# A tile of its own for the weights of q and k, and the first unit's maxima among the last projections

## The chip, the core and the metric

The kernel runs on one core of one Trainium2 chip. A core has five engines that run beside each other, each through its own list of instructions in order: TensorE (PE, with its weight loads as PEld), VectorE (DVE), ScalarE (ACT), GpSimd (POOL) and SyncE (SP), which here issues nearly all DMAs. The metric is the device time of one execution in microseconds (us), the median of several runs. In the profile a tile is named by its program name (`khat`, `rl`, `pm`); nearly all instructions are recorded through one helper, so the profile gives line 76 for all of them, and one goes by tiles.

## The reference

Two independent results are put side by side, 448 columns each, for 2048 positions, all in 32-bit floats:

```python
P = exp((A * dt)[:, :, None] * pos)          # A complex, 448 channels x 256 states
K = 2 * einsum("dn,dnl->dl", C, P).real      # a convolution kernel of 2048 for each channel
y = irfft(rfft(u_t, 4096) * rfft(K, 4096))[:, :, :2048] + u * D_skip

q, k, v = split(x @ wqkv)                    # 16 heads of 28
p = softmax(q @ k.T * 28 ** -0.5)
b = (p @ v) @ wo
```

## The kernel before, in words

**Opening stage** (lines 213 to 565). It makes two things and writes both to DRAM. One is q, k and v: x is turned on PE in four chunks of 512 rows (`transposes`, line 433), split into a rounded part `xh` and a rest `xl`, and multiplied by the weights, split in the same way. A q or k projection (`qk_proj`, line 443) is twelve matmuls of 512 columns into one bank of PSUM, for one chunk and one group of four heads; ScalarE and VectorE then split the result into `hl`, which is written out. A v projection (`v_proj`, line 475) is twelve matmuls too, evacuated by ScalarE. There are 12 projections a chunk, 48 in all; all take their bank from one ring of three (`w_tile`, line 126). The other thing is the *seeds*: for eight blocks of 56 channels (`seeds`, line 314) exponentials and sines on ScalarE, reductions and small products on VectorE (`g_first`, line 400), factors on POOL (`factors`, line 381). These make the tables from which the main loop builds powers of exp(A dt).

A seed block is thirteen steps, and a block begins every four slots (`SP`), so that there are 41 slots; the projections are spread over the first 37 (`PW`). Loads for the main loop are put into slots by `ahead` and the constants `A0`, `A1`, `KW` (line 44). In this stage the written order is only a priority: a scheduler orders the instructions of each engine when the kernel is built. The chip then follows that order, engine by engine.

The weights of q and k lie in the tile `khat` (`k0_t`, lines 135 and 233), in which the first group's keys are to lie later: four parts of 1 MB, one for each head slot `j`, each loaded by four DMAs of 256 KB (`load_k`, line 146). The weights of group `j` lie in part `j`, so a part can be loaded when all the projections of its group are done. x, v's weights and small tiles lie in the pool `y_p` (line 218).

**First maxima** (lines 537 to 562). Softmax takes an upper bound of each row's maximum off the scores. For a unit (four heads and 512 queries; there are 16 units) it is found by scores on PE, with one difference of keys for each pair of chunks (`kdif`): max(a, b) = b + relu(a - b). For the first unit this is done after the stage, 16 times: five matmuls into two tiles of two banks, a Relu of 128x1024 on ScalarE and an add-and-maximum of 128x1024 on VectorE. One matmul takes the negated q (`nq`, made by POOL). The 16 maxima are then turned by PE, split by VectorE into `mh` and written into spare rows of `qhat` by a DMA (`max_end`, `max_put`, lines 199 and 207), so that the score matmul subtracts them itself.

**Main loop** (from line 878). 256 steps, 16 for each unit, with an order that is written out by hand and kept as written (`ORDER`): scores, exponentials and sums of one unit, the maxima of the next, and the convolution's work in between. It reads the first seeds (`sdb`), `qhat` and `khat` at its start.

Pools lie in memory as stacks, some from the left, some from the right end: a pool that opens where another was closed waits for the users of the old tiles. A tile of a pool with several buffers waits for the last use of the buffer that it gets.

Of the kernel before, what the change touches and what calls it, by code (L numbers as in the profile page):

```python
# [8 lines left out]
F32 = mybir.dt.float32  # L9
# [8 lines left out]
L = 2048  # L18
# [3 lines left out]
DH = 28  # L22
# [21 lines left out]
A0, A1, KW = 26, 34, (33, 35, 36)  # L44
# [47 lines left out]
def body(ctx, tc, a, out):  # L92
# [41 lines left out]
    k0_p = pool(k0_st, "k0_p", side="right")  # L134
    k0_t = k0_p.tile([128, HG, L], F32R, name="khat")
# [10 lines left out]
    def load_k(g, j, p):  # L146
        if j == 0:
            t = k0_t if g == 0 else p.tile([128, HG, L], F32R, name="khat")
# [64 lines left out]
    with ExitStack() as st:  # L213
        sst, xst, wst, mst, psx, psm = (ExitStack() for _ in range(6))
# [3 lines left out]
        y_p = pool(wst, "y_p", side="right")  # L218
# [17 lines left out]
        nc.gpsimd.memset(k0_t[:CK].rearrange("p g (n e) -> p (g n) e", e=32)[:, :, DH:].bitcast(F32), 0.0)  # L236
# [16 lines left out]
        def load_nat(o):  # L253
            nats[o] = s_p.tile([PO, 4, 256], F32, name="nat", bufs=2)
# [178 lines left out]
        def transposes(c):  # L433
            for k in range(NCK):
                pt = ps_t.tile([128, CQ], F32, name="pt")[:CK]
                for t in range(4):
                    nc.tensor.transpose(pt[:, t * 128:(t + 1) * 128], xns[c, t // 2][:, t % 2, k * CK:(k + 1) * CK], ident)
                xh[k] = x_p.tile([CK, CQ], F32R, name="xh", bufs=XB)
                xl[k] = x_p.tile([CK, CQ], F32R, name="xl", bufs=XL)
                nc.scalar.activation(xh[k], pt, AF.Copy)  # L440
                nc.vector.tensor_tensor(xl[k], pt, xh[k].bitcast(F32), ALU.subtract)
# [47 lines left out]

        work = []  # L490
# [23 lines left out]
        for j, t in enumerate(KW):  # L514
            ahead[t].append(lambda j=j: load_k(0, j, k0_p))

        def project():

            e = work.pop(0)() if work else None
            while pend:  # L520
                pend.pop(0)()
            if e:
                pend.append(e)

        for t in range(n_stage):
# [4 lines left out]
            if t + 1 == PW:  # L530
                project()
                wst.close()
                load_k(0, HG - 1, k0_p)
                load_q(1)
                for c in range(NQ):
                    load_v(0, c)
        xst.close()
        psx.close()
        m_p = pool(mst, "m_p")
        ps_2 = pool(psm, "ps_2", 4, PSUM)  # L540
        nq = m_p.tile([128, HG, CQ], F32R, name="nq")
        m_u[0, 1] = q_p.tile([128, HG * 4], F32, name="m1", bufs=2)
        for i in range(16):
            j, t = divmod(i, 4)
            ts = slice(t * 128, (t + 1) * 128)
            q, kt = q_u[0][:, j, ts], kt_g[0][j]
            if t == 0:
                nc.gpsimd.tensor_scalar(nq[:, j], q_u[0][:, j].bitcast(F32), -1.0, None, op0=ALU.mult)
            pd, pb = (ps_2.tile([128, 2, CQ], F32, name="p2") for _ in range(2))
            kb = kt.rearrange("p (c s n) -> p c s n", c=NQ, s=2)[:, :2, 1, :]  # L550
            mm = nc.tensor.matmul
            mm(pd[:, 0], q, kd_g[0, j], start=True, stop=True)
            mm(pd[:, 1], q, kt[:, 2 * CQ:3 * CQ], start=True, stop=False)
            mm(pd[:, 1], nq[:, j, ts], kt[:, 3 * CQ:], start=False, stop=True)
            mm(pb[:, 0].rearrange("p (c n) -> p c n", c=2), q, kb, start=True, stop=True)
            mm(pb[:, 1], q, kt[:, 3 * CQ:], start=True, stop=True)
            rl = m_p.tile([128, 2, CQ], F32, name="rl2", bufs=2)
            nc.scalar.activation(rl, pd, AF.Relu)
            nc.vector.tensor_tensor_reduce(rl, pb, rl, 1.0, -3.0e38, ALU.add, ALU.max, m_u[0, 1][:, i:i + 1])
        nc.scalar.activation(half_pi[:1], half_pi[:1], AF.Exp)  # L560
        max_end(0, ps_2.tile([128, 2, CQ], F32, name="p2")[:, 0])
        max_put(0)
        psm.close()
        mst.close()
# [12 lines left out]
    k_pools = [k0_p, kq_p]  # L577
# [580 lines left out]
```

## Time and profile before

| what | value |
| --- | --- |
| median of three runs | 1303.82 us (1302.89 to 1305.15) |
| the profiled execution | 1307.74 us |
| its span, first to last instruction | 1305.7 us |
| mean clock of PE | 0.976 |
| PE busy from 0 to 180 us, in stretches of 20 us | 12.06 to 18.74 us |
| PE busy from 260 to 300 us | 39.45 us |
| bytes moved by DMA | 205.28 MB, mean 157 GB/s |

The span is the profile's own, and the time beside it is that of the same execution. Engine rows give a start, a duration, the operation, out<-in, and in brackets the idle time before it and what ended it. The chain of waits is followed back from the last instruction: each piece is released by the one before it.

### The profile page before, as it was taken

The numbers are of one execution on the slowest core, as the hardware profiler recorded it, in microseconds if no ns is written. First come the engines' busy times: TensorE is split into PE (matmuls) and PEld (weight loads), VectorE is DVE, ScalarE is ACT, GpSimd is POOL, SyncE is SP. The second block draws the span as 40 slices with busy tenths as digits, with TensorE's granted clock in tenths as the row PEclk, the third lists the DMA queues.
The fourth block names the chain that finished last, engine by engine and source line by source line (L and its number), as shares of the span: only waits on it lengthen the run. The fifth ranks groups of instructions, "written<-read, shape, count | busy, mean of one in ns | idle before, by whom it ended". The sixth has DMA issues, their size and how long they took to land.

```text
span 1305.7 us, 32148 instructions
## 1 busy us (share of the span) xinstructions
PE 1228.7 (94%) x12193; PEld 695.7 (53%) x12193; DVE 907.0 (69%) x2001; ACT 980.3 (75%) x2046; POOL 865.9 (66%) x684
## 2 busy tenths in 40 slices
PE   6888877799999999999999999999997999999998
PEld 5766755355555555555555555555554555545333
DVE  5676656677777787777788888888986555636111
ACT  4877875588888888888788888888886666756463
POOL 2677654478888788888769999999995221424421
PEclk9989887799999999999999999999999999999999
DMA  6677679735866455468634232743324453647666
GB/s 202 207 273 257 218 259 271 212 66 136 185 147 142 109 149 157 142 169 231 162 104 105 56 83 62 157 111 78 82 59 139 146 158 136 203 142 238 202 161 175
DMA packets 200082, 205.28 MB, mean 157 GB/s; under 512 B 95992, under 2 KB 158520, under 8 KB 197880
## 3 DMA queue, kind: packets, MB, share of 16 engines
q1 hardware_dynamic: 199864, 203.22, 56.1%
q8 instruction: 96, 1.57, 0.5%
q14 instruction: 58, 0.48, 0.1%
q10 hardware_dynamic: 64, 0.02, 0.0%
HBM read 120.74 MB, written 82.18 MB: 155 GB/s over the span
## 4 chain that ended last, share of the span: by engine, by line
PE 72%; POOL 8%; ACT 7%; DVE 5%; DMA 4%; issue 4%; SPq 0%; ACTq 0%; POOLq 0%
PE pm L76 39%; PE pss L76 16%; PE po L76 16%; POOL sg L76 2%; POOL e L76 2%; DMA khat<-k 2%; POOL tri L76 2%; ACT tri L76 1%; ACT sg L76 1%; DVE mx L76 1%; POOL p L76 1%; ACT L76 1%; ACT p L76 1%; POOL eu L76 1%; DVE rl L76 1%
## 5 line engine op out<-in xcount | busy, mean ns | idle before, releaser
L76 ACT ACTIVATE p<-pss 128x512 f32<-128x512 f32 x1024 | 560.4, 609 | 109.9 <-PE pss L76 105.9
L76 PE MATMUL pss<-qhat,khat 128*128 128x512 f32 x1024 | 405.7, 402 | 4.0 <-DMA qhat<-mh 2.2
L76 DVE TENSOR_REDUCE mx<-pm 128x1 f32<-128x512 f32 x480 | 308.3, 683 | 121.2 <-PE pm L76 119.5
L76 PE MATMUL pm<-khat,qhat 128*128 128x512 f32 x720 | 314.4, 437 | 6.1 <-ACT rl L76 3.5
L76 POOL TENSOR_TENSOR e<-e,sdb 128x256 f32<-128x256 f32 x168 | 202.0, 1203 | 108.7 <-ACT e L76 67.2
L76 PE MATMUL po<-p,v 128*32 128x512 f32 x2048 | 271.0, 597 | 0.0
L76 POOL TENSOR_TENSOR e<-e,eu 128x256 f32<-128x256 f32 x168 | 248.3, 1478 | 13.2
L76 PEld LDWEIGHTS pm<-khat,qhat 128*128 128x128 f32 x720 | 135.4, 188 | 206.4 <-ACT p L76 47.0
L76 PEld LDWEIGHTS pss<-qhat,khat 128*128 128x128 f32 x1024 | 191.2, 189 | 52.5 <-ACT p L76 13.8
L76 DVE CUSTOM_DVE_ANT_0 rl<-pm,rl 128x512 f32<-128x512 f32 x240 | 165.3, 689 | 70.0 <-ACT rl L76 67.7
L76 POOL TENSOR_TENSOR eu<-e,sdb 128x256 f32<-128x256 f32 x168 | 202.3, 1204 | 0.0
L76 POOL TENSOR_TENSOR p<-pr,pr 64x448 f32<-64x448 f32 x64 | 73.2, 1144 | 155.6 <-PE pm L76 122.3
L76 DVE TENSOR_TENSOR g<-g,zg 128x128 f32<-128x128 f32 x392 | 162.0, 413 | 3.6
L76 ACT ACTIVATE rl<-pm 128x512 f32<-128x512 f32 x240 | 145.3, 605 | 7.7 <-issue 4.1
L76 PE MATMUL pm<-xh,khat 112*128 112x512 f32 x256 | 89.7, 431 | 19.6 <-DVE hl L76 10.6
L76 PE MATMUL pm<-kdif,qhat 128*128 128x512 f32 x240 | 97.0, 404 | 1.7 <-DVE pr L76 1.1
L76 DVE TENSOR_TENSOR zg<-g,zg 128x128 f32<-128x128 f32 x224 | 88.0, 393 | 5.3
L76 PEld LDWEIGHTS pm<-e,g 128*32 128x32 f32 x3584 | 56.9, 110 | 49.2 <-issue 15.7
L76 PE MATMUL pm<-e,g 128*32 128x64 f32 x3584 | 73.6, 223 | 8.7 <-POOL e L76 8.7
L76 ACT ACTIVATE y<-pm 128x448 f32<-128x448 f32 x48 | 26.5, 553 | 59.7 <-PE pm L76 39.1
L76 PEld LDWEIGHTS pm<-xh,khat 112*128 112x128 f32 x256 | 51.0, 205 | 35.9 <-DVE hl L76 12.6
L76 DVE TENSOR_TENSOR pr<-pm,ub 128x448 f32<-128x448 f32 x64 | 37.0, 619 | 46.9 <-PE pm L76 37.7
(133 smaller groups left out, 1491.6 us busy)
## 6 DMA issues: line engine op xcount, KB each, us to landing
sdb<-sd SPq DMA_DIRECT2D x56, 336.0 KB
khat<-k SPq DMA_DIRECT2D x64, 256.0 KB
qhat<-q SPq DMA_DIRECT2D x64, 256.0 KB
sd<-sg SPq DMA_DIRECT2D x8, 1456.0 KB
k<-hl SPq DMA_DIRECT2D x16, 512.0 KB
q<-hl SPq DMA_DIRECT2D x16, 512.0 KB
v<-v SPq DMA_DIRECT2D x32, 256.0 KB
mw<-in_mw SPq DMA_DIRECT2D x16, 512.0 KB
```

The lines of the kernel that those rows point to most:

```text
L76: i = f(*args, **kw)
```

## The change

- The weights of q and k get a tile `w` of their own in a new pool on the left side. The pool of the first keys, `k0_p`, is opened only in the course of the last projections, after `y_p` has been closed, and lies where `y_p` was.
- The rests `xl` of three of the four parts of x lie in tiles of v's pool instead of a pool of their own; a `nat` tile is 128 rows high, so that the negated q can lie in it.
- In the last chunk the keys of the first group are projected first, then v, then the others.
- From the 41st projection on, a plan `MG` gives for each the part of the keys to load and the first unit's maxima to compute after it: parts 2, 3, 0, 1 after projections 41 to 44, and from 43 on two maxima after each; the rest follows after the stage.
- Each maximum is done in two halves of 512 columns: each has a tile of one bank for the difference (`pt`, two buffers, that of the transposes) and one of the ring of three for the added part, a Relu of 128x512, and an add-and-maximum of 128x512 into a column of its own. One more reduction joins the halves at the end.
- The differences of keys and the first q are loaded in earlier slots (`A0` 26 to 18, `A1` 34 to 28).

```diff
-A0, A1, KW = 26, 34, (33, 35, 36)
+A0, A1 = 18, 28
+MG = {41: (2, ()), 42: (3, ()), 43: (0, (8, 9)), 44: (1, (10, 11)), 45: (None, (12, 13)), 46: (None, (14, 15)), 47: (None, (0, 1)),
+      48: (None, (2, 3)), 49: (None, (4, 5)), 50: (None, (6, 7))}
...
-    k0_p = pool(k0_st, "k0_p", side="right")
-    k0_t = k0_p.tile([128, HG, L], F32R, name="khat")
...
+        w_p = pool(wst, "w_p")
+        y_p = pool(yst, "y_p", side="right")
...
-        w_g = k0_t[:CK].rearrange("p g (i s k h e) -> p i s k g h e", i=2, s=2, k=NCK, h=HG)
+        w_t = w_p.tile([CK, HG, L], F32R, name="w")
+        w_g = w_t.rearrange("p g (i s k h e) -> p i s k g h e", i=2, s=2, k=NCK, h=HG)
...
+        xls = [v_p.tile([128, NK // NQ, HG, 32], F32, name="v", bufs=5).rearrange("p t h e -> p (t h e)")[:CK].bitcast(F32R) for _ in range(3)]
+        xls.append(x_p.tile([CK, CQ], F32R, name="xl"))
...
+        def max_group(i):
+
+            j, t = divmod(i, 4)
+            ts = slice(t * 128, (t + 1) * 128)
+            if not nqs:
+                m_u[0] = q_p.tile([128, HG, 4, 3], F32, name="mx", bufs=2)
+            if t == 0:
+                if j % 2 == 0:
+                    nq = s_p.tile([128, 4, 256], F32, name="nat", bufs=2).rearrange("p (j a) n -> p j (a n)", j=2).bitcast(F32R)
+                    nqs[j], nqs[j + 1] = nq[:, 0], nq[:, 1]
+                nc.gpsimd.tensor_scalar(nqs[j], q_u[0][:, j].bitcast(F32), -1.0, None, op0=ALU.mult)
+            q, kt = q_u[0][:, j, ts], kt_g[0][j]
+            kb = kt.rearrange("p (c s n) -> p c s n", c=NQ, s=2)[:, :2, 1, :]
+            mm = nc.tensor.matmul
+            for h in range(2):
+                pd, pb = ps_t.tile([128, CQ], F32, name="pt"), w_tile()
+                if h == 0:
+                    mm(pd, q, kd_g[0, j], start=True, stop=True)
+                    mm(pb.rearrange("p (c n) -> p c n", c=2), q, kb, start=True, stop=True)
+                else:
+                    mm(pd, q, kt[:, 2 * CQ:3 * CQ], start=True, stop=False)
+                    mm(pd, nqs[j][:, ts], kt[:, 3 * CQ:], start=False, stop=True)
+                    mm(pb, q, kt[:, 3 * CQ:], start=True, stop=True)
+                rl = kd_p.tile([128, CQ], F32, name="rl", bufs=2)
+                nc.scalar.activation(rl, pd, AF.Relu)
+                nc.vector.tensor_tensor_reduce(rl, pb, rl, 1.0, -3.0e38, ALU.add, ALU.max, m_u[0][:, j, t, h:h + 1])
+
+        def first_maxima(n):
+
+            j, ts = plan.pop(n, (None, ()))
+            if j is not None:
+                if not k0:
+                    yst.close()
+                    k0.append(pool(k0_st, "k0_p", side="right"))
+                load_k(0, j, k0[0])
+            for i in ts:
+                groups.remove(i)
+                max_group(i)
...
-            jobs = v_jobs + jobs if c == NQ - 1 else jobs + v_jobs
+            jobs = jobs[:1] + v_jobs + jobs[1:] if c == NQ - 1 else jobs + v_jobs
...
-        for j, t in enumerate(KW):
-            ahead[t].append(lambda j=j: load_k(0, j, k0_p))
...
+            first_maxima(n_work - len(work))
...
-                load_k(0, HG - 1, k0_p)
...
+            elif t + 1 > PW:
+                first_maxima(n_work + t + 1 - PW)
+        while groups:
+            max_group(groups.popleft())
```

More of the change, by code (lines that the diff above doesn't have):

```diff
@@ L146, in load_k @@
     def load_k(g, j, p):
-        if j == 0:
-            t = k0_t if g == 0 else p.tile([128, HG, L], F32R, name="khat")
+        if g not in kt_g:
+            t = p.tile([128, HG, L], F32R, name="khat")
             kt_g[g] = [t[:, i] for i in range(HG)]
@@ L213, in body @@
     with ExitStack() as st:
-        sst, xst, wst, mst, psx, psm = (ExitStack() for _ in range(6))
+        sst, xst, wst, yst, psx = (ExitStack() for _ in range(5))
+        k0 = []
         t_p = pool(sst, "t_p")
@@ L438, in transposes @@
                 xh[k] = x_p.tile([CK, CQ], F32R, name="xh", bufs=XB)
-                xl[k] = x_p.tile([CK, CQ], F32R, name="xl", bufs=XL)
+                xl[k] = xls[k]
                 nc.scalar.activation(xh[k], pt, AF.Copy)
@@ L488, in v_proj @@
             return evac
+        nqs, plan = {}, dict(MG)
+        groups = collections.deque([j * 4 + t for j in (2, 3, 0, 1) for t in range(4)])
+        def max_group(i):
[33 more added lines that the diff above has]
+                max_group(i)
         work = []
@@ L536, in body @@
                     load_v(0, c)
+            elif t + 1 > PW:
+                first_maxima(n_work + t + 1 - PW)
+        while groups:
+            max_group(groups.popleft())
+        nc.scalar.activation(half_pi[:1], half_pi[:1], AF.Exp)
+        m_u[0, 1] = q_p.tile([128, HG * 4], F32, name="m1", bufs=2)
+        nc.vector.tensor_reduce(m_u[0, 1], m_u[0].rearrange("p a b c -> p (a b) c")[:, :, :2], axis=AX.X, op=ALU.max)
+        max_end(0, ps_t.tile([128, CQ], F32, name="pt"))
+        max_put(0)
         xst.close()
         psx.close()
[L539 to L564, printed above, removed]
         sst.close()
```

7 lines of the change are left out of this document (3 added, 4 removed).

## The prediction

> **What bounds the kernel now.** I read the page first: the span, the busy time of each engine, and PE's share slice by slice.
>
> ```profile
> span 1305.7 us, 32148 instructions
> PE 1228.7 (94%) x12193; PEld 695.7 (53%) x12193; DVE 907.0 (69%) x2001; ACT 980.3 (75%) x2046; POOL 865.9 (66%) x684
> PE   6888877799999999999999999999997999999998
> ```
>
> From the ninth slice on (a slice is 32.6 us) TensorE is busy nine tenths and more: the main loop. I compared the order of instructions in the two kernels: from the main loop's first instructions to the end it is the same on all five engines. So only the opening stage, some 245 us, can change. I read that stage in windows (stretch, length, busy PE, PEld, DVE, ACT, POOL with their counts, clock, DMA share, GB/s), and then in the chain of work that ended last.
>
> ```profile
> 180.00:190.00 10.00, 4.84 (x12) 3.84 (x13) 8.55 (x13) 4.68 (x9) 5.32 (x5) 0.66 0.44 167
> 190.00:200.00 10.00, 7.26 (x25) 5.38 (x24) 1.44 (x2) 9.91 (x13) 4.38 (x3) 0.83 1.03 291
> 200.00:210.00 10.00, 2.86 (x8) 2.03 (x7) 5.38 (x11) 2.57 (x8) 7.84 (x8) 0.66 1.08 263
> ```
> ```profile
> 208.44 9.86 DMA khat<-k
> 218.32 10.46 DMA khat<-k
> 228.92 3.26 PE p L76 x12
> ...
> 235.65 0.02 DVE m L76
> ...
> 236.38 5.56 DMA qhat<-mh
> ...
> 242.00 2.99 DMA sdb<-sd
> ...
> 245.15 0.63 ACT e L76
> ```
>
> From 180 to 210 one engine at a time is near full and the others wait for it. From 208.44 to 228.79 the chain is the load of the first keys. The last maximum is done at 235.67, and the main loop's first work on ScalarE starts at 245.15, 9.5 us later. The change acts on what comes before 235.67.
>
> **The change part by part.** *What it removes.* The first keys no longer wait for weights in the same tile. Without their loads the old maxima would still have to run:
>
> ```profile
> L76 DVE CUSTOM_DVE_ANT_0 rl<-p,rl 128x1024 f32<-128x1024 f32 x16 | 19.2, 1224 | 8.3 <-ACT rl L76 7.8
> L76 DVE DVE_READ_ACCUMULATOR2_ANT m<- 128x1 f32 x16 | 1.3, 83 | 0.0
> L76 ACT ACTIVATE rl<-p 128x1024 f32<-128x1024 f32 x16 | 16.3, 1026 | 10.9 <-PE p L76 10.4
> ```
>
> 16 x (1.224 + 0.083) = 20.9 us of VectorE from about 208 would end near 229: the loads cost at most 235.7 - 229 = 7 us. What is gained beyond that must come from maxima beside projections.
>
> *What it adds.* 32 halves of 128x512 stand for 16 maxima of 128x1024. The main loop has both instructions:
>
> ```profile
> L76 DVE CUSTOM_DVE_ANT_0 rl<-pm,rl 128x512 f32<-128x512 f32 x240 | 165.3, 689 | 70.0 <-ACT rl L76 67.7
> L76 ACT ACTIVATE rl<-pm 128x512 f32<-128x512 f32 x240 | 145.3, 605 | 7.7 <-issue 4.1
> L76 ACT ACT_TABLE_LOAD x4 | 5.1, 1283 | 0.1
> ```
>
> VectorE: 32 x (0.689 + 0.083) = 24.7 us, 3.8 more. ScalarE: 32 x 0.605 = 19.4, 3.0 more. Matmuls (80) and negations of q (four) stay. The new order also holds 23 activation table loads instead of 17: 6 x 1.283 = 7.7 us more on ScalarE, because Exp and Sin alternate inside the later seed blocks. The Trainium skill, ScalarE: Activation LUTs, section "Table sets: the hidden batching unit", asks to batch activations by table set, which speaks against this order; the price here is the row's, so the rule alters nothing in the sum.
>
> *What it moves, and the waits.* Each engine takes its instructions in the order written, so I followed the new order from the place where it departs, with durations and distances of these rows:
>
> ```profile
> 136.42 1.13 ACT L76 ACTIVATE tri<-tri,half_pi 128x1008 f32<-128x1008 f32 x1
> 143.34 0.69 DVE L76 TENSOR_TENSOR hl<-pm,hl 128x512 fp32r<-128x512 f32 x1
> 144.09 0.47 PE L76 MATMUL pm<-vh,xh 112*128 112x448 f32 x1 [1.97 <-DVE hl L76]
> 148.17 1.28 ACT L76 ACT_TABLE_LOAD   x1
> 153.17 1.12 ACT L76 ACTIVATE tri<-tri,half_pi 128x1008 f32<-128x1008 f32 x1
> 163.47 0.63 PE L76 MATMUL pm<-xh,khat 112*128 112x512 f32 x2
> 166.04 0.40 PE L76 MATMUL pm<-xl,khat 112*128 112x512 f32 x1
> 175.73 1.12 ACT L76 ACTIVATE tri<-tri,half_pi 128x1008 f32<-128x1008 f32 x1
> 176.45 2.27 SPq L76 DMA_DIRECT2D kdif<-kd  x2
> 179.53 0.40 PE L76 MATMUL pm<-xl,khat 112*128 112x512 f32 x1
> 185.16 1.22 PE L76 MATMUL pm<-xh,khat 112*128 112x512 f32 x2 [5.23 <-DVE hl L76]
> 189.82 0.39 PE L76 MATMUL pm<-xl,khat 112*128 112x512 f32 x1
> 191.94 2.69 SPq L76 DMA_DIRECT2D khat<-k  x4
> 201.43 0.56 DVE L76 TENSOR_TENSOR sg<-pn,tri 128x224 f32<-128x224 f32 x1 [2.12 <-POOL tri L76]
> 205.06 0.55 DVE L76 TENSOR_TENSOR sg<-sg,px 128x224 f32<-128x224 f32 x1
> L76 POOL TENSOR_SCALAR nq<-qhat 128x512 fp32r<-128x512 f32 x4 | 5.9, 1492 | 2.2 <-DMA qhat<-q 2.2
> ```
>
> (1) The fifth seed's cosines (136.42) come about 2.6 us later, behind two more table loads. The split of the third chunk's last q projection (143.34) now stands on VectorE behind all nine small products of that seed (201.43 to 205.61 in the rows of the eighth: 4.2 us) instead of among them. I put it at 150. PE's v projection that waits for this bank (144.09) goes with it.
> (2) That projection (3.0 warm, 163.47 to 166.44; 5.0 cold, 185.16 to 190.21), the last chunk's transposes and the first keys' projection take about 7 us, to 157. ScalarE's split of these keys stands ahead of the sixth seed's sines. That group took 6.1 us (148.17 to 154.29); with two more loads it takes 8.7 or 9. Its cosines end at 166, where they ended at 154.3.
> (3) The four v projections need banks that ScalarE frees between these pieces; the third evacuation stands behind the seventh seed's cosines. From one seed's cosines to the next it took 16.7 us (137.55 to 154.29) and 22.6 (to 176.85). I take 19, the shorter one with two loads: 185. Only then can PE begin the second key projection. Before had done four of the last chunk's eight by 179.9; here it is two. SP is in that line too: the third write of v stands ahead of the first key load, so that goes out near 186 (before 191.94), and the next three behind the fourth write, near 195. At 10 us for each megabyte of keys, as in the chain's two rows, the second is there by 205, the last by 225, ahead of the maxima that need them. So I cost the loads at nothing; without that cover they are worth the 7 us above.
> (4) After the long gap this projection runs cold: 5.0, to 190.5. The fourth v evacuation, whose bank the first maximum needs, stands on ScalarE behind table loads, the eighth seed's sine and the key split: between 0.7 and 7 us of pieces, I take 4.5: 195. The negated q comes from POOL behind that seed's product, 1.5 more: 196.5. Here the maxima start.
> (5) Five projections and 32 halves remain, and they share three banks of PSUM: a projection waits for VectorE to release a half's bank, and the next half for the split of a projection. A block is one projection 3.0, four halves 4 x 0.772 = 3.1, and the hand-over before VectorE can start, a matmul 0.4 and ScalarE's 0.6: 7.1 us. Five blocks are 35.5: 232. Twelve halves are left, 12 x 0.772 = 9.3: 241.3. The eighth seed's pieces stand in the same queues, 4.2 us on VectorE and some 6.5 on ScalarE; between 0 (all in gaps) and 10.7 (in series) I take 5: 246.3. Against 235.7 that is **10.6 us later**.
>
> *The rest at nothing.* The join is one reduction of 32 numbers a partition, under the 0.7 of a 128x512 maximum. The hand-over of 9.5 us stays: the first seed load still stands behind the maxima's write. v's last two tiles hold x until the last projection; the unit's first eight key steps hide their loads, and without that each costs about the 3 us of the seed load. The keys' differences and q are loaded earlier, on an SP that stands idle between; its issue row (176.45) bounds them at 1.1 us each if it doesn't. Memory places give the main loop no new wait: its waits are the same.
>
> The profiled execution took 1307.74 us, 2.0 outside its span and 3.9 above the median of 1303.82. With 10.6 it would be 1318.3, and a median **1314**.
>
> **The rivals.** *Overlap works.* Faster: VectorE never waits from 190.5 on. Its work is 24.7 + six splits of 0.7 + 4.2 = 33.1 us: the last maximum at 223.6, 12 us sooner, 1292. For it: no other engine has more work, and the keys are there. Against it: two buffers each for scores and results, and windows like 180 to 210. It decides where VectorE is busy more than 33.1 of 45.2 us, 73%; at 80% the end is 232, 4 us sooner, 1300. *Even.* The seed falls into gaps and each block saves a microsecond: 236, 1304. *Worse.* All of (5) in series with the seed: 252, 16 us, 1320; with a cold projection in some blocks 1325. *The keys decide after all*, so that the change doesn't do what it says: three loads from 195 at 10 us each and a delay behind the other writes, last at 230 to 235, then the last group's maxima: 238 to 243, 1306 to 1311.
>
> The clock is another rival's ground: it was 0.66 from 200 to 210 after PE had idled, and PE kept busier could stay at 1. The Trainium skill, TensorE: Matmul & The Clock Gate, section "HAM oscillation", puts the danger at gaps above about 3.4 us, and by it most blocks would run warm; my blocks are priced warm already, so by it nothing comes off the sum.
>
> **How the numbers follow.** About 0.2%, 2.6 us, is what a measurement of this kernel can tell from no change. Forecast (3 to 15 us later, the keys' rival in it): 0.55. Worse: 0.10. Even: 0.11. Overlap in part, 1294 to 1301: 0.14; in full: 0.10. So faster 0.24, same 0.11, slower 0.65. Leaving out the full overlap and the far end of worse the range is 1295 to 1325; the forecast's own is 1307 to 1319.
>
> **What would show it.** (1), (2): the sixth seed's cosines end near 166 and not 154. (3): PE idles for microseconds before 185, and the first key load is issued near 186. (4): few maxima before 195. (5): VectorE busy about 60% from 196 to a last maximum near 246. If the sixth cosines end by 158, or the second key projection starts by 178, (1) to (3) are wrong and overlap takes over; if PE has done the last projection by 225, (5) is.

## The result, and the profile after

| what | before | after |
| --- | --- | --- |
| median | 1303.36 us (1302.15 to 1305.15) | 1326.89 us (1325.92 to 1327.63) |
| the profiled execution | 1307.74 us | 1326.86 us |
| its span | 1305.7 us | 1324.7 us |
| first instruction of the main loop on ScalarE (`e<-sdb`) | 245.15 us | 266.45 us |
| from there to the end of the span | 1060.5 us | 1058.2 us |

The ratio is 1.0179, with a 95% interval from 1.0161 to 1.0197: 23.5 us slower by the medians, 19.0 by the spans, since the profiled execution of before lay 4.4 above its median. The prediction, 1314 (1295 to 1325), had the sign and less than half of the size. The opening stage takes 21.3 us more, and all of the loss is there. The main loop is 2.3 us shorter, but that is no gain of the change: over the executions of all the kernels below, whose main loop is the same but for where a few loads stand, it takes 1057.2 to 1060.9 us.

The page of after, its span, busy times and PE by slices:

```profile
span 1324.7 us, 32207 instructions
...
PE 1232.1 (93%) x12193; PEld 697.3 (53%) x12193; DVE 911.6 (69%) x2034; ACT 991.3 (75%) x2068; POOL 863.5 (65%) x684
...
PE   6887748689999999999999999999998899999998
```

PE does the same work as before. The low slices are still the first ones, and lower: the sixth (166 to 199 us) has four tenths where before had seven, the eighth (232 to 265) six for seven. The same stretches as in the prediction's windows, and those behind them (length, busy PE, PEld, DVE, ACT, POOL with counts, clock, DMA share, GB/s):

```profile
180.00:190.00 10.00, 4.10 (x10) 3.23 (x11) 5.04 (x6) 8.53 (x10) 9.18 (x6) 0.54 0.41 105
190.00:200.00 10.00, 3.20 (x9) 2.26 (x8) 8.05 (x13) 4.88 (x9) 7.34 (x8) 0.67 0.28 64
200.00:210.00 10.00, 9.80 (x39) 7.45 (x39) 4.41 (x13) 5.27 (x9) 2.62 (x2) 0.93 1.06 262
210.00:220.00 10.00, 8.95 (x29) 5.95 (x27) 3.19 (x9) 5.21 (x8) 0.00 (x0) 0.83 1.03 300
220.00:230.00 10.00, 6.87 (x20) 4.71 (x20) 4.26 (x12) 8.06 (x10) 7.25 (x5) 0.83 0.66 219
230.00:240.00 10.00, 5.36 (x13) 2.89 (x12) 6.68 (x16) 4.77 (x12) 0.41 (x1) 0.77 0.42 159
```

From 180 to 200 ScalarE and POOL, then VectorE are near full with the seventh and eighth seed block, and PE runs some 35% of the time. From 200 to 240, where maxima and projections were to fill each other's gaps, VectorE has 3.2 to 6.7 us of work in each 10. It was full in none of them.

The engine rows of after that answer to the prediction's steps: the sixth and the eighth seed block's cosines on ScalarE, PE's long waits and the end of each of the five projections that stand between maxima, and SP's key loads and last writes:

```profile
163.94 1.12 ACT L78 ACTIVATE tri<-tri,half_pi 128x1008 f32<-128x1008 f32 x1
...
225.09 1.13 ACT L78 ACTIVATE tri<-tri,half_pi 128x1008 f32<-128x1008 f32 x1
```
```profile
185.90 1.22 PE L78 MATMUL pm<-xh,w 112*128 112x512 f32 x2 [7.77 <-ACT v L78]
198.35 0.80 PE L78 MATMUL pm<-khat,qhat 128*128 128x512 f32 x1 [6.80 <-ACT v L78]
204.46 0.40 PE L78 MATMUL pm<-xl,w 112*128 112x512 f32 x1
207.54 0.63 PE L78 MATMUL pm<-xh,w 112*128 112x512 f32 x2
210.09 0.40 PE L78 MATMUL pm<-xl,w 112*128 112x512 f32 x1
212.44 0.51 PE L78 MATMUL pm<-khat,qhat 128*128 128x512 f32 x1 [0.79 <-DVE mx L78]
214.71 0.81 PE L78 MATMUL pm<-xh,w 112*128 112x512 f32 x2
218.81 0.39 PE L78 MATMUL pm<-xl,w 112*128 112x512 f32 x1
229.67 0.40 PE L78 MATMUL pm<-xl,w 112*128 112x512 f32 x1
235.12 0.52 PE L78 MATMUL pm<-khat,qhat 128*128 128x512 f32 x1 [3.59 <-DVE hl L78]
243.43 0.39 PE L78 MATMUL pm<-xl,w 112*128 112x512 f32 x1
```
```profile
186.48 1.99 SPq L78 DMA_DIRECT2D khat<-k  x4
198.90 2.02 SPq L78 DMA_DIRECT2D khat<-k  x4
...
206.55 3.98 SPq L78 DMA_DIRECT2D khat<-k  x4
256.64 0.37 SPq L78 DMA_DIRECT2D sd<-qhat  x1
257.06 0.56 SPq L78 DMA_DIRECT2D sd<-sg  x1
257.67 3.91 SPq L78 DMA_DIRECT2D sdb<-sd  x3
```

The end of the opening in after's chain of waits (before's pieces at this place began at 235.65):

```profile
252.70 0.60 DVE rl L78
...
254.30 2.28 DMA qhat<-mh
...
257.67 8.71 DMA sdb<-sd
...
266.45 0.13 ACT e L78
```

The last maximum ends at 253.30 (before 235.67). Then the maxima's write lands at 256.58; only there does SP issue the eighth block's two writes and, behind them, the first seed load, which takes 8.71 us where before took 2.99.

The clock that goes with PE's rows, in stretches of 2 us (busy PE, clock, DMA share, GB/s):

```profile
212.00:214.00 2.00, 1.44 (x4) 1.00 1.06 391
...
216.00:218.00 2.00, 2.00 (x6) 0.50 1.12 284
```

The third, fourth and fifth projection run in part at half clock: 4.5 us from the row at 214.71 to the end of that at 218.81, and 4.2 and 4.6 for the next two (in the last, one matmul of a half stands between them), where the second took 2.95 (207.54 to 210.49).

### The profile page after: what moved, and what is told of

It is laid out like the page before. It is cut to its first block, busy times and chain, and to the rows that moved or that the text cites. A ratio compares the mean times of both kernels' runs of the same rounds, so it can differ in the third digit from the quotient of the medians.

```text
span 1324.7 us, 32207 instructions
## 1 busy us (share of the span) xinstructions
PE 1232.1 (93%) x12193; PEld 697.3 (53%) x12193; DVE 911.6 (69%) x2034; ACT 991.3 (75%) x2068; POOL 863.5 (65%) x684
## 4 chain that ended last, share of the span: by engine, by line
PE 71%; DVE 4%; POOL 3%; issue 2%; ACT 2%; DMA 1%; SPq 0%; ACTq 0%; POOLq 0%
PE pm L78 39%; PE pss L78 16%; PE po L78 16%; POOL e L78 2%; DVE mx L78 1%; POOL p L78 1%; ACT p L78 1%; POOL eu L78 1%; DMA sdb<-sd 1%; DVE rl L78 1%; ACT rl L78 1%; DVE zg L78 0%; PE pt L78 0%; DVE mh L78 0%; DVE g L78 0%
## 5 line engine op out<-in xcount | busy, mean ns | idle before, releaser
L78 PE MATMUL pm<-khat,qhat 128*128 128x512 f32 x752 | 329.5, 439 | 26.8 <-ACT rl L78 9.3
L78 PEld LDWEIGHTS pm<-khat,qhat 128*128 128x128 f32 x752 | 142.1, 189 | 232.6 <-ACT p L78 52.0
L78 DVE CUSTOM_DVE_ANT_0 rl<-pm,rl 128x512 f32<-128x512 f32 x272 | 186.9, 689 | 89.0 <-ACT rl L78 78.0
L78 PEld LDWEIGHTS pss<-qhat,khat 128*128 128x128 f32 x1024 | 191.3, 189 | 49.5 <-ACT p L78 13.8
L78 PE MATMUL pm<-xh,w 112*128 112x512 f32 x256 | 91.9, 441 | 22.2 <-ACT v L78 9.8
L78 PEld LDWEIGHTS pm<-xh,w 112*128 112x128 f32 x256 | 52.8, 212 | 37.9 <-ACT v L78 10.6
```

Source lines behind the costliest of these rows:

```text
L78: i = f(*args, **kw)
```

## The experiments

The theory after the result had four parts: (a) the **earlier loads** (`A0`, `A1`) alter the scheduler's order of the seeds, with six more table loads; (b) **ScalarE's v evacuations** hold PE up before 198; (c) maxima and projections **take turns** instead of overlapping; (d) the **hand-over** suffers from what stands on SP ahead of the seed load. Rivals: the halves are dear in themselves, the late key loads, or one late seed block that holds everything. None of the kernels leaves work out. In the diffs, `MG*` is the plan with the key loads one projection later (parts 2, 3, 0, 1 after 42 to 45).

| run | median us (range) | before, same call | ratio [95% interval] |
| --- | --- | --- | --- |
| e1_late_slots | 1318.18 (1317.70 to 1319.74) | 1303.79 | 1.0110 [1.0082, 1.0137] |
| e2_early_loads_alone | 1314.23 (1313.69 to 1316.49) | 1303.79 | 1.0081 [1.0053, 1.0109] |
| e3_maxima_after_stage | 1325.30 (1323.71 to 1326.55) | 1303.79 | 1.0161 [1.0133, 1.0190] |
| e4_halves_alone | 1301.42 (1300.50 to 1302.84) | 1303.79 | 0.9981 [0.9968, 0.9994] |
| e5_late_slots_v_first | 1319.90 (1317.33 to 1322.04) | 1303.88 | 1.0121 [1.0101, 1.0141] |
| e6_v_on_vectore | 1325.73 (1325.18 to 1326.89) | 1303.88 | 1.0168 [1.0152, 1.0183] |
| e7_seeds_ahead_of_v | 1320.28 (1316.48 to 1323.07) | 1303.88 | 1.0123 [1.0101, 1.0144] |
| e8_v_first_maxima_after | 1309.73 (1307.55 to 1310.84) | 1303.88 | 1.0042 [1.0027, 1.0056] |
| e9_seed_write_early | 1329.81 (1328.57 to 1330.56) | 1303.68 | 1.0196 [1.0179, 1.0213] |
| e10_e5_seed_write_early | 1323.69 (1323.36 to 1324.77) | 1303.68 | 1.0154 [1.0138, 1.0169] |
| e11_e8_seed_write_early | 1309.54 (1307.62 to 1310.68) | 1303.68 | 1.0042 [1.0027, 1.0057] |
| e12_e4_seed_write_early | 1307.21 (1305.97 to 1309.11) | 1303.68 | 1.0026 [1.0014, 1.0038] |
| e13_late_slots_and_seeds_ahead | 1313.97 (1312.59 to 1314.42) | 1303.97 | 1.0070 [1.0053, 1.0087] |
| e14_own_bank | 1319.86 (1318.81 to 1321.04) | 1303.97 | 1.0117 [1.0102, 1.0132] |
| e15_halves_behind_the_stage | 1308.74 (1308.51 to 1311.30) | 1303.97 | 1.0039 [1.0026, 1.0052] |
| e16_e4_seeds_ahead_of_v | 1301.44 (1299.64 to 1303.91) | 1303.97 | 0.9982 [0.9973, 0.9992] |
| e17_e15_key_loads_later | 1308.61 (1306.49 to 1310.20) | 1304.71 | 1.0029 [1.0019, 1.0039] |
| e18_e10_fine_interleave | 1317.57 (1316.18 to 1321.02) | 1304.71 | 1.0101 [1.0085, 1.0118] |

Below, the *last maximum* is the end of the last add-and-maximum on VectorE, and the time *from the turned maxima* runs from the first `mh` row on VectorE to the first `e<-sdb` on ScalarE: 9.12 us in before, 12.46 in after. It leaves out the turning itself.

**The earlier loads: e1 (after with the keys' differences in late slots) and e2 (before with the earlier loads).** e1 also loads heads 2 and 3 first, and keeps q's early slot.

```diff
 e1, to after:
-A0, A1 = 18, 28
+A0, A1 = 26, 28
-    load_kd(0, i // 2, range(...))
+    load_kd(0, (i // 2 + 2) % HG, range(...))
 e2, to before:
-A0, A1, KW = 26, 34, (33, 35, 36)
+A0, A1, KW = 18, 28, (33, 35, 36)
```

> Kernel after, with the loads of the keys' differences back in the old slots (from 26, those of heads 2 and 3 first); the order on ScalarE then holds 17 activation table loads instead of 23. Theory (the earlier loads alone turn the seeds' order round, and this makes steps 1 to 4 late): the sixth seed's cosines end near 155 instead of 165, the maxima start some 8 us sooner, the last maximum comes near 245 and the time is 1319, 8 below after. Rival (the lateness comes from the v projections behind the first keys in the last chunk, whatever the seeds' order): PE waits for ScalarE's v evacuations as before, 1325 to 1327.

> Kernel before, with only the two constants of the change (18 and 28) for the loads of the keys' differences and of the first q. Its order has 23 table loads. Theory: six table loads at 1.283 us, 7.7 us, in a stretch where ScalarE sets the pace; the sixth seed's cosines come 8 us later, of which the first keys' loads at the end pass on 5 to 8: 1308 to 1311. Rival: ScalarE has room for them, 1303 to 1305.

e1 takes 8.7 us off after and e2 puts 10.4 on before. The table loads up to 260 us, after first and then e1, and e1's cosines of the sixth block:

```profile
L78 ACT ACT_TABLE_LOAD x23 | 29.5, 1283 | 1.1 <-PEq L1175 0.7
```
```profile
L78 ACT ACT_TABLE_LOAD x17 | 21.8, 1283 | 1.0 <-PEq L1175 0.7
```
```profile
151.72 1.13 ACT L78 ACTIVATE tri<-tri,half_pi 128x1008 f32<-128x1008 f32 x1
```

With the later slots there are 17 table loads again, and the sixth block's cosines start at 151.72 instead of 163.94 (before 153.17); e2 has 23 and starts them at 160.01. So this part is shown from both sides, and e2 has neither the new tile nor the new maxima. The Trainium skill, ScalarE: Activation LUTs, section "Table sets: the hidden batching unit", asks for activations of one table set together; e1 and e2 agree in sign. That the six table loads (7.7 us) are most of the 8.7 is not shown: e9 below has 17 of them too, with the sixth block's cosines at 158.29, and is 2.9 us slower than after. What else the new order costs isn't told apart from them.

**v's evacuation: e6 (on VectorE in the last chunk) and e5 (e1 with v ahead of the keys).**

```diff
 e6, to after, last chunk only:
-nc.scalar.activation(vs[:, :, :DH], pp[...], AF.Copy)
+nc.vector.tensor_copy(vs[:, :, :DH], pp[...])
 e5, to e1, with MG*:
-jobs = jobs[:1] + v_jobs + jobs[1:] if c == NQ - 1 else jobs + v_jobs
+jobs = v_jobs + jobs if c == NQ - 1 else jobs + v_jobs
```

> Kernel after, with the last chunk's four v evacuations on VectorE instead of ScalarE. Theory (step 3 and 4: a bank that PE needs stands on ScalarE behind the seventh seed): the two waits of 7.8 and 6.8 us on ScalarE's v go, the maxima start near 190 instead of 198, the time is 1318 to 1321. Rival (PE would only wait for the next thing, the keys or VectorE): 1325 to 1328.

> As e1 (late slots), and in the last chunk v is projected first again, as in before; each part of the keys is loaded one projection later, the maxima of the plan stay. Theory (after the seeds' order, the rest of the lateness is PE waiting for ScalarE's v evacuations in the last chunk): PE is busy from 170 to 190 as in before, the maxima start near 188, the last one comes by 238 to 240 and the time is 1309 to 1312. Rival (maxima and projections in one order stall each other and the eighth seed, whatever comes before): 1316 or more, no better than 2 below e1.

Neither gains: e6 is 1.2 us below after, inside the ranges, e5 1.7 above e1, inside theirs. In e6 PE's wait ahead of the second key projection is this:

```profile
182.53 1.22 PE L78 MATMUL pm<-xh,w 112*128 112x512 f32 x2 [5.20 <-DVE v L78]
```

The wait has changed its engine and shrunk from 7.77 to 5.20, but the next one, ahead of the first maximum, has grown from 6.80 to 10.61, for v's evacuation on VectorE: PE goes on at 198.63 where after does at 198.35. In e5 that place is at 192.22 (e1 190.31), behind a wait of 6.63 us for the first keys. So in both PE only waits for the next thing. The ScalarE waits of steps (3) and (4) are seen; what an earlier start of the maxima would be worth was not tested, since neither kernel has one.

**The hand-over: e7 (v's loads moved behind the first seed loads) and e13 (e1 and e7 together).**

```diff
-                for c in range(NQ):
-                    load_v(0, c)
...
     for b in range(3):
         load_sd(b)
+    for c in range(NQ):
+        load_v(0, c)
```

> Kernel after, with v's four loads issued behind the first three seed loads instead of ahead of them; by this the eighth seed's writes and the first seed load no longer stand on SP behind the maxima's write. Theory (of the hand-over's 13.1 us some 4 to 5 are this order): from the last maximum to the first seed's powers 8 to 9 us, 1322. Rival (the seed load is slow because of the megabytes of loads and writes around it, in any order): 1325 to 1327.

> e1 and e7 together on the kernel after (late slots; v's loads behind the seed loads). If the two parts are separate, 8.7 and 6.6 add: 1311 to 1313. Rival (both shift one and the same wait): no better than 1317.

SP in e7, at the place of after's rows 256.64 to 257.67:

```profile
248.77 0.38 SPq L78 DMA_DIRECT2D sd<-qhat  x1
...
250.61 9.58 SPq L78 DMA_DIRECT2D sdb<-sd  x3
```

The eighth block's writes go out 8 us sooner, ahead of the maxima's write, with the maxima turned at nearly the same time as in after (254.54, after 253.99). So they need nothing of that write; in after SP held them 5.0 us for it (the list of SP's waits names `qhat<-mh`). From the turned maxima it takes 6.86 us instead of 12.46, and the time is 6.6 below after. In e13 the two parts give 12.9 of 15.3: they mostly add. What is left against before is 10.0 us, and it lies ahead of the last maximum (246.78; before 235.67).

**The halves by themselves: e4 (before with halves) and e16 (e4 with e7's edit).**

```diff
+for h in range(2):
+    pd, pb = (ps_2.tile([128, 2, CQ], F32, name="p2")[:, 0] for _ in range(2))
...
-nc.scalar.activation(rl, pd, AF.Relu)                      # 128x1024
-nc.vector.tensor_tensor_reduce(rl, pb, rl, ..., m_u[0, 1][:, i:i + 1])
+    nc.scalar.activation(rl, pd, AF.Relu)                  # 128x512
+    nc.vector.tensor_tensor_reduce(rl, pb, rl, ..., m_u[0][:, j, t, h:h + 1])
```

> Kernel before, with the sixteen maxima of 1024 columns done as 32 halves of 512 at the same place. Theory: VectorE has 3.8 us more to do and is what the end waits for: 1307. Rival (halves bring a hand-over of their own each, and are the cause): 10 us or more, 1313 or above. If the keys' loads cover them: 1304.

> As e4 (before, maxima in halves), with v's loads behind the first three seed loads. In e4 the first seed load is already ahead of the maxima's write, but the megabyte of v's loads goes beside the keys' and the writes. Theory (the hand-over's order matters only where the eighth block's writes stand behind the maxima's): no change from e4, 1300 to 1303. Rival (less traffic ahead of the maxima's write and the seed load): 1297 to 1299.

Both are faster than before, by 2.4 and 2.5 us, 0.2%: little, but outside both intervals. The end of the opening in e4's chain, and SP there:

```profile
232.07 0.97 PE p L76 x3
233.06 0.61 ACT rl L76
233.69 0.69 DVE rl L76
...
236.04 4.79 DMA qhat<-mh
```
```profile
234.42 6.18 SPq L76 DMA_DIRECT2D sdb<-sd  x3
```

In e4 PE and ScalarE alternate, 0.97 + 0.61 us, 1.65 with what lies between, for each pair of halves. Before's wholes, on VectorE:

```profile
219.03 1.23 DVE L76 CUSTOM_DVE_ANT_0 rl<-p,rl 128x1024 f32<-128x1024 f32 x1
...
227.87 1.23 DVE L76 CUSTOM_DVE_ANT_0 rl<-p,rl 128x1024 f32<-128x1024 f32 x1
```

The eight from 219.03 to 227.87 start 1.26 apart; then VectorE waits 1.61 us, until 230.71, behind the last keys (in the prediction's chain they land just ahead of PE's piece at 228.92). So a pair of halves does take longer, by more than the prediction's 3.8 us in 16, but it starts sooner (first reduction at 206.85, before 212.79) and no longer waits for keys: the last maximum ends at 234.38, before 235.67, no more than one execution's opening differs from another's (the last chunk's `xh` begins at 125.95 in before, 123.84 in e4, 122.49 in after). The gain is in the hand-over: the first seed load goes out at 234.42 instead of before's 242.00, ahead of the maxima's write and not behind it, and from the turned maxima it takes 6.15 us instead of 9.12. Why the finer maxima let it go is not told apart. With e16 the 6.15 become 2.38, but then the matmuls wait for the same write, and the time stays.

**Maxima after the stage: e3 (after) and e8 (e5).** Both keep the halves and the early key loads, without the tuples of maxima in the plan.

```diff
 e3:
+MG = {41: (2, ()), 42: (3, ()), 43: (0, ()), 44: (1, ())}
 e8:
+MG = {42: (2, ()), 43: (3, ()), 44: (0, ()), 45: (1, ())}
```

> Kernel after, with the keys' loads as they are but all 32 halves after the stage. Theory (halves and projections stall each other through three banks and the eighth seed): the five projections end by about 222 instead of 244, the halves take 25 us behind them, last maximum near 248, 1321. Rival (the overlap is worth most of what it was meant for, and the time was lost earlier): the halves are added to what is there, last maximum near 262, 1333 or more.

> As e5, with all 32 halves after the stage: what is left of the change is the tile of its own, the early key loads and the halves. Theory: the projections end near 207 as in before, the keys are there, 32 halves take 25 us, last maximum at 233 to 235, hand-over 8 to 13: 1303 to 1308. Rival (the new places or the early key loads cost time by themselves): above 1312.

In after it makes no difference beyond the ranges (1.6 us less), in e5's order it gives 10.2. In neither pair did the mixture of maxima and projections make the kernel faster. But its price is not where the theory had it, in turns between maxima and projections. In e5 and e8 the last maximum comes at the same time, 246.4 and 245.8 us; what differs is the way from the turned maxima, 12.05 and 2.09 us. In e8 the projections are done long before the maxima, and SP issues the eighth block's writes and the first seed load while VectorE is still busy with maxima:

```profile
234.11 2.34 SPq L78 DMA_DIRECT2D sdb<-sd  x3
```

In e8 SP issues the last projection's write at 221.46, 24 us ahead of the last maximum, in e5 at 236.83, 10 us ahead, and the loads and writes of the hand-over follow it: the first seed load goes out at 250.38, behind the last maximum. So nearly all of the 10.2 us is the hand-over. In after the mixture even brings the last maximum 10 us forward (253.3; e3 263.3), and the hand-over takes it back (12.46; e3 2.09). That e3's last maximum is so late goes with its eighth block, which stays where it was (cosines 224.35, after 225.09), with the 32 halves behind it; in e8 it comes at 206.75 (e5 216.30).

**One late seed block? e9 to e12 write each block's tables (`put_g`) two steps sooner, in after, e5, e8 and e4.**

```diff
-... [g_copies], [], [put_g]]
+... [g_copies, put_g], [], []]
```

> Kernel after, with the write of each seed block's second table (sg, 1456 KB) put right behind the copies that complete it, two slots earlier; the order then holds 17 table loads again, and the sixth block's write stands on SP behind one part of the keys instead of three. Theory, formed after e1 to e8 (the sixth block's write stands behind the keys' loads on SP, and the eighth block's first sine needs its buffer, one of two): the eighth block's sines start by 207 instead of 217, the last maximum comes near 244, 1315 to 1319. Rival (the eighth block is late because ScalarE is taken by other work, and the buffer is free by then): 1323 to 1327.

> As e5, with the seed writes two slots earlier; the sixth block's write then stands on SP ahead of all key loads. Theory of the seed write: the eighth block's first sine at about 193 instead of 209, last maximum at 235 to 239 instead of 246, 1307 to 1312. Rival (maxima among projections cost this by themselves, through the banks): 1316 or more.

> As e8, with the seed writes two slots earlier, ahead of all key loads. Theory of the seed write: the eighth block's first sine at 190 to 194 instead of 199.8, the last maximum near 238 instead of 245.8, 1301 to 1304. Rival (what is late in e8 is the halves after the stage): 1308 to 1311.

> As e4 (before with halves), with the seed writes two slots earlier. In before that write is out at 176 and nothing waits for it, the keys' loads set the end: by the theory of the seed write 1300 to 1303, no difference from e4. Rival (the seeds' order itself, 15 table loads instead of 17, is worth time): 1297 or less.

The eighth block's cosines do come sooner, by 12.0, 18.3 and 8.3 us in e9, e10 and e11, and the time is 2.9 and 3.8 us longer and the same; e12 loses 5.8. This theory fell. PE waits somewhere else, in e12 9.84 us for q (`qhat<-q`, up to 213.56), in e10 for the first keys (and 10.09 us more at 207.69 for ScalarE):

```profile
194.71 0.77 PE L78 MATMUL pm<-khat,qhat 128*128 128x512 f32 x1 [12.28 <-DMA khat<-k]
```

e10 is of use all the same: from 207.69 on no seed is in the way of its projections and halves. VectorE's splits there, and a window:

```profile
223.12 0.75 DVE L78 SCALAR_TENSOR_TENSOR hl<-pm,kones,hl 128x512 fp32r<-128x512 f32 x1
230.50 0.69 DVE L78 TENSOR_TENSOR hl<-pm,hl 128x512 fp32r<-128x512 f32 x1 [1.21 <-ACT hl L78]
237.76 0.75 DVE L78 SCALAR_TENSOR_TENSOR hl<-pm,kones,hl 128x512 fp32r<-128x512 f32 x1 [1.31 <-ACT hl L78]
```
```profile
220.00:230.00 10.00, 9.68 (x38) 6.53 (x37) 5.47 (x15) 5.28 (x10) 0.00 (x0) 1.00 1.03 338
```

A block of one projection and four halves takes 7.4 and 7.3 us at full clock, beside the prediction's 7.1, with VectorE half idle. With the ring as it is the overlap isn't there even when no seed disturbs it.

**What makes them take turns? e14 gives the projections from the 44th on a bank of their own, e18 issues a half after every third matmul of a projection; both stand on e10.**

```diff
 e14:
-            pp = w_tile()
+            pp = w_tile(0 if n_work - len(work) >= 44 else None)
-    pd, pb = ps_t.tile([128, CQ], F32, name="pt"), w_tile()
+    pd, pb = ps_t.tile([128, CQ], F32, name="pt"), w_tile(1 + h)
 e18, in the loop of a projection's matmuls:
+                if fine:
+                    fine.popleft()()
```

> As e10, but from the 44th projection on the projections have one bank of the three to themselves, and the halves alternate between the other two. In e10 the splits of the last projections come 7.2 us apart, near the sum of a projection and four halves. Theory of step 5 (the turn is taken through the shared banks): a block takes 5 to 6 us, the last maximum is 6 to 10 us sooner than 251.5, 1314 to 1318. Rival (PE's written order takes the turns, a projection's twelve matmuls in one run, and the banks don't matter): blocks of 7 us as before, 1322 to 1326.

> As e10, but each half of a maximum is issued between three matmuls of a projection and the next three, so that on PE no projection of the last five is one run of twelve. Theory (the written order of PE takes the turns: VectorE idles through a run of twelve): splits of the last projections 5 to 6 us apart instead of 7.2, last maximum 5 to 8 us sooner, 1315 to 1319. Rival (banks and the chain from matmul over Relu to VectorE pace the halves anyway): 1322 to 1326.

e14 gains 3.8 us, less than the theory of the shared bank gave. The end of its chain:

```profile
241.97 0.68 DVE rl L78
243.65 4.29 DMA qhat<-mh
...
249.94 9.98 DMA sdb<-sd
```

With a bank of its own for the projections only one half is left behind the last split (241.37), where e10 has nine behind its own (243.53): the last maximum ends at 242.65, and the turned maxima start at 243.34 where e10 has 252.31. But that is not overlap. VectorE stands idle beside each of the three last projections in e14, for 2.3 to 3.0 us, while PE does the twelve matmuls in one run; two of these places:

```profile
220.74 0.69 DVE L78 CUSTOM_DVE_ANT_0 rl<-pm,rl 128x512 f32<-128x512 f32 x1 [2.30 <-PE pm L78]
228.47 0.69 DVE L78 CUSTOM_DVE_ANT_0 rl<-pm,rl 128x512 f32<-128x512 f32 x1 [3.03 <-ACT rl L78]
```

From VectorE's first half to its last there are 34.8 us and three projections in e14, 45.1 and five in e10; the halves themselves are 32 x 0.772 = 24.7 of both. So a projection among halves costs 3.4 us instead of 4.1, and by this reckoning most of the 9 us comes from two projections that stand ahead of the first half (207.81, e10 206.53), where PE waits a good part of the time in both (12.28 and 10.09 us in e10, 17.36 in e14). The hand-over takes most of it back: 16.65 us from the turned maxima instead of 11.22, with the seed load behind the late writes again. e18 gains 6.1: the last maximum is 3.4 sooner, with one projection fewer among the halves, and the hand-over, 8.36, is 2.9 shorter; its blocks are hardly shorter (splits at 217.26, 224.26, 231.52 and 237.30). So neither the shared banks nor PE's runs of twelve alone make them take turns: with either one taken away a projection still stops the halves. e14's and e18's edits together were not run, nor e14 with e7's.

**What remains with the maxima behind the stage: e15 (e8 with the halves in banks opened after the stage) and e17 (e15 with later key loads).**

```diff
 e15, to e8:
+        xst.close()
+        psx.close()
+        ps_2.append(pool(psm, "ps_2", 8, PSUM))
 e17, to e15:
+MG = {44: (2, ()), 46: (3, ()), 47: (0, ()), 48: (1, ())}
```

> As e8 (tile of its own, late slots, v first, early key loads), but the 32 halves get banks that open only when the stage's are closed, so that none of them can stand ahead of a seed. In e8 the first half's Relu stood on ScalarE ahead of the eighth block and waited 8.8 us for the keys. Theory: the eighth block is that much sooner, projections end near 207, the last maximum near 234, as in e4: 1299 to 1303. Rival (the early key loads or the new places delay the projections by themselves): 1307 to 1311 as e8.

> As e15, but the first keys' parts are loaded after projections 44, 46, 47 and 48 instead of 42 to 45: on SP the sixth block's write then stands ahead of all of them, as in before, and they stand between the writes of the last projections. Theory (the early key loads cost e15 its 7 us, through that write): the eighth block's cosines near 196 instead of 205.7, projections end near 207, last maximum near 234: 1300 to 1303. Rival (the new places of w, x and the keys delay the projections by themselves): 1306 to 1311.

e15 is 1.0 below e8, inside the ranges, so the old banks weren't it. e17 brings the eighth cosines from 205.74 to 196.80 and the last maximum from 244.2 to 236.1, near before's 235.7, as its theory had said: early key loads ahead of the seeds' writes on SP delay the last maximum by 8 us. In e15 the eighth block's first sine waits 10.85 us for such a write (`sd<-sg`), in e17 0.97. The time is the same, 1308.6, because the hand-over, from the turned maxima, grew from 2.1 to 12.0. SP in e17:

```profile
239.00 0.37 SPq L78 DMA_DIRECT2D sd<-qhat  x1
...
240.03 3.92 SPq L78 DMA_DIRECT2D sdb<-sd  x3
```

It is after's picture: the block's writes behind the maxima's write, the seed load behind them, landing at 248.7. e17 with e7's edit, which should keep both gains, was not run.

## Why the prediction came out as it did

**That only the opening stage changes** held: from `e` to the end of the span it is 1060.5 and 1058.2, within what other executions show.

**By how much it was off.** The sum gave 1318.3 for the profiled execution, and 3.9 came off because before's lay that far above its median. After's lies at its median. So the sum itself missed by 8.5 us (1326.9 profiled) and the median by 12.9; the steps below account for the profiled executions.

**Steps (1) to (3)** held: the split of (1) came at 147.08 (150), the sixth block's cosines ended at 165.06 (166), the seventh's at 185.42 (185), the first key load went out at 186.48 (186), the next only at 198.90 ("near 195"), and no marked wait of PE is for keys. **Step (4)** was 1.9 short: 198.35 instead of 196.5.

**Step (5) failed in its size.** From 198.35 to the end of the fifth projection, 243.82, it took 45.5 us: 6.5, 5.6, 8.7, 10.9 and 13.8 by the ends of the projections' last matmuls. The prediction had 35.5 and 5 for the eighth seed's pieces, 40.5. Blocks without seed pieces were priced well (6.5 and 5.6 here, 7.4 and 7.3 in e10, for 7.1), but the reason given, banks in one ring, is only a part of it: with a bank of their own (e14) a projection among halves costs 3.4 us instead of 4.1, and VectorE still idles beside it. Two terms were too small. "My blocks are priced warm already": three of the five projections ran partly at clock 0.50, 1.5, 1.3 and 1.6 us over the second one's 2.95 (0.4 of the last is the half's matmul), some 4 in all. And the seed's pieces (217 to 234 on ScalarE, POOL and VectorE): the 10 us above 35.5, less these 4, leave some 6 for 5, after the first two blocks had saved 2; so they were worth about 8 of the 10.7 "in series". The row at 235.12 is such a place: PE waits 3.59 us for a split that stood on VectorE behind the seed's products. The remaining twelve halves took 9.5 (9.3). So the last maximum came 7.0 us later than predicted: 5.0 from the blocks, 1.85 from step (4), 0.2 from the twelve halves. The shares of clock and seed are worked out from the rows, not tested by a run.

**"The hand-over of 9.5 us stays" failed**: 13.15, 3.7 more. The prediction looked at the order of SP, which indeed had the seed load behind the maxima's write, but not at what stands right ahead of it: the eighth block's writes, 2.4 MB together, which in before had gone out at 232.66 and 233.82, and in after waited for the maxima's write. 7.0 + 3.7 are the 10.7 us by which the opening missed; less the main loop's 2.3 they are the 8.5 of the sum, to 0.1. That the order on SP is what costs is shown by e7 (6.6 us).

**"The keys' differences and q are loaded earlier, on an SP that stands idle"**, at nothing or 1.1 us each, failed. e1 and e2 price the earlier slots at 8.7 and 10.4. The six table loads stood in the sum's working as 7.7 us, but as a cost of the new order, of which the earlier loads were thought to be innocent. So the prediction had the delay of the sixth block right and its cause not. This put no error into the total, since the table loads were in it.

**The price of the halves**, 3.8 us, was of the right sign for the piece (in e4 1.65 us for a pair, in before 1.26 for a whole) and of the wrong one for the kernel: e4 is 0.9981 of before [0.9968, 0.9994].

**The rivals.** "Overlap works" decided at 73% of VectorE; it was busy 32 to 67% in the four windows from 200 to 240, and without seeds (e10) the blocks don't shorten; no run has the maxima beside the projections, e14 (another bank) and e18 (shorter runs on PE) each alone don't do it. "Worse", all of (5) in series (252, 1320) and cold projections in some blocks (1325), names most of what came, some 8 of the seed's 10.7 us and some 4 of cold; it had 0.10, and lacked the hand-over. "The keys decide" did not come: the last key load was issued at 206.55 and no wait for it stands in the chain. The clock rival went the other way. Ahead of the third projection PE's longest marked wait since 206 was 0.79 us (212.44); it was busy 1.44 of the 2.00 us around it, at clock 1.00, and from 216 to 218 it had 0.50. The Trainium skill, TensorE: Matmul & The Clock Gate, section "HAM oscillation", speaks of gaps above about 3.4 us; of the waits marked ahead of the three slow projections (0.79, 1.27 and 3.59 us) only the last is one. Here several short waits went before a half clock as well.

**The account of the 23.5 us**: the earlier loads 8.7 (e1) and the hand-over 6.6 (e7), 12.9 together (e13); the other 10.0 lie ahead of the last maximum. Taking the maxima out from between the projections does not bring it forward (e5 246.4, e8 245.8), later key loads do, by 8 us (e15 244.2, e17 236.1), but that was measured with the maxima behind the stage. With the maxima between, no run has the later key loads, and there seeds that come sooner did not help (e9, e10). So for after itself the cause of these 10 us is argued and not shown.

## What to carry to other kernels

Filling one stage's gaps with another's work pays only if the two really run beside each other. Here they shared banks and PE's order, and taking away either one was not enough (e14, e18): price such a block as a sum, put whatever else stands in those queues on top, and price it at the slow clock where PE has had to wait. And see what the filling does to the end of the stage: where the projections ended late, among the maxima, the next stage's loads stood behind the last maximum (12.05 us from the turned maxima in e5, 2.09 in e8). When loads move in a kernel that a scheduler orders, compare the table loads and the order of the engines with only that move made; it can cost more than the move's own subject. And look at what is issued just ahead of the first load of the next stage: in after two writes, 2.4 MB together, came late there, and an order that sends them sooner gave 6.6 us (e7).

## What the runs showed that was not expected

- A seed load of the same size took 2.99 us in before and 8.71 in after, where it was issued 0.6 us behind the second of two large writes. It goes the same way elsewhere: 8.68 in e17 and 9.98 in e14, also 0.6 behind it, and 2.91 in e18, 9 us behind it (before 8 us).
- SP held a write for a DMA that it doesn't depend on (5.0 us, `qhat<-mh`): e7's order lets the same write go before it. Why it was held is not shown.
- The clock fell to 0.50 behind several waits of about a microsecond each (after, 212 to 218 and 220 to 228).
- Halves are slower by the pair (1.65 us in e4, 1.26 for a whole in before) and let the main loop start sooner.
- Maxima between projections and maxima behind them end at the same time in e5 and e8; the first way costs 10.2 us more, by what then still stands on SP.
- Seeds that come 8 to 18 us sooner (e9 to e11) moved the end by nothing or made it later.
